# Three PSUM places for a second-layer tile, block products in single-bank tiles, normalisation one tile later, halves of 384 and 512 tokens

## The chip, the cores and the metric

The kernel runs on one core of a Trainium2 chip. The metric is the device time of one execution in microseconds; before the change three runs gave a median of 462.89 us (462.61 to 463.26). The engines are named as the profile names them: PE (TensorE, matrix products; PEld is its weight load), DVE (VectorE), ACT (ScalarE), POOL (GpSimd) and SP (SyncE, which here issues DMAs). PSUM is the memory that PE writes its products to; it has eight banks of 512 float32 columns, and DVE and ACT read it.

## The reference

Three stages, all in float32, on 2 x 448 = 896 tokens of width 768:

```python
scores = cap * tanh(scale * q @ k.T / cap); attn = softmax(scores)      # 2 x 12 heads of 64
x = (attn @ v)                                                         # 896 x 768
h = x @ moe_w_in                                                       # 768 -> 2048
x = (s * relu(h)**2 + b) @ moe_w_out                                   # 2048 -> 768
h = x @ moe2_w_in                                                      # 768 -> 1024
solu = h * exp(h - max(h)) / (sum(exp(h - max(h))) + 1e-9)
ln = (solu - mean) / sqrt(var + 1e-6) * g_ln
out = ln @ moe2_w_out                                                  # 1024 -> 768
```

The weights come in as float64 and are turned into float32 on the chip.

## The kernel before

Each matrix is split into a high part in a shortened format (fp32r) and the remainder, and one product is three matmuls: high x high, high x low, low x high (`mm3`, L374 to L377). The tile framework puts the instructions of each engine in one fixed order and adds the semaphore waits; every engine then runs its own list strictly in order.

Attention comes first and is not changed. In the first feed-forward layer the tokens stand along the columns and are cut in two halves, of 510 and 386 tokens (`M0`, L399, `HALVES`): for each of 16 blocks of 128 hidden units there is one product per half (`in_unit`), whose result ACT turns into relu squared. Then `split_g` (L402) makes the high and low part of s times that; two extra columns on the first half (512 columns in all) carry b, so that column `M0` of a result is the constant to add.

The second product of that layer is done in two sweeps (`sweep`, L1068): output blocks `dc` 0 and 1, then 2 to 5, each in one PSUM bank per half, summed over the 16 hidden blocks. At a sweep's end `evac` (L1093) moves each bank to SBUF as a high part (ACT, L1115) and a low part (DVE, L1118). The target `y` is laid out by tiles of 128 tokens; 510 is not a multiple of 128, so each half takes two pieces: 384 and 126 columns, and 2 and 384. PE may start a product in a bank of the next sweep when all pieces of the block that was there have been read.

The last layer goes by seven tiles of 128 tokens. `h2(t)` makes the tile's 1024 columns of h in one place of two banks; there are two such places (`ps_h`, L1188), so tile t+2 waits until DVE's product `so = h * rs * e` (L1210), the last reader, has finished tile t. `epilogue` (L1199) is a chain through three engines: DVE max (L1200), ACT exp (L1204), DVE sum and reciprocal, DVE `so` and its sum (L1210), ACT square (L1216), POOL variance, power -0.5 and minus mean times that (L1217, L1220, L1221), and ACT normalise (L1222). Beside it DVE and ACT convert the last weights `w2o` and form sums of their blocks (`block_sums`, L808), which `weights.pump(11)` interleaves, tile by tile.

The output product treats tile 0 alone (`first_out`, L1281) and the other tiles in pairs (`pair_out`, L1326): tiles t and t+1 share seven half-size products of 4 x 3 matmuls instead of eight, from sums and differences of rows (`pair_rows`, L1295) and of weight blocks. The results x, y, z, w of the products are columns of two tiles of two banks each, `xy` and `zw`, from the same places as h; DVE adds them up (L1350) and the rows are stored by SP's queue (`store`, L1377). `in_turn` fixes the order of PE here.

Of the kernel before, what the change touches and what calls it, by code (L numbers as in the profile page):

```python
# [10 lines left out]
F32 = mybir.dt.float32  # L11
# [3 lines left out]
AF = mybir.ActivationFunctionType  # L15
ALU = mybir.AluOpType
# [4 lines left out]
def full(ap):  # L21

    return ap.bitcast(F32)
# [14 lines left out]
def tile_softcap_attention__relu2__solu(  # L38
# [39 lines left out]
    def psum(name, bufs):  # L78
        return tc.tile_pool(name=name, bufs=bufs, space=PSUM, reuse_waits="tile")
# [116 lines left out]
    def layers(ctx, general):  # L196
# [199 lines left out]

        M0 = 510  # L399
        HALVES = (slice(0, M0), slice(M0, NT))  # L400

        def split_g(fc, part):  # L402
# [625 lines left out]
        gsp = left.enter_context(sb("gs"))  # L1028
        pairs = ([], [])
        for n in range(GSB):  # L1030
            m = 512 if n % 2 == 0 else NT - M0
            gh, gl = (gsp.tile([P, m], F32R, name=f"g{x}{n}") for x in "hl")
            pairs[n % 2].append((gh, gl))
            if n % 2 == 0:
                ends = slice(M0, M0 + 2)
                nc.gpsimd.tensor_copy(gh[:, ends], b_t.to_broadcast([P, 2]))
                nc.gpsimd.tensor_tensor(
                    out=gl[:, ends], in0=b_t.to_broadcast([P, 2]), in1=full(gh[:, ends]),
                    op=ALU.subtract,
                )  # L1040
# [38 lines left out]
        def sweep(dcs, banks, wname, used, pumps):  # L1079
            ahead = dict(split_ahead)  # L1080
            split_ahead.clear()

            def get(fc):
                if fc < KF and fc not in ahead:
                    ahead[fc] = [split_g(fc, b) for b in range(B)]

            def unit(fc, dc, b):
                wh, wl = wname(fc)
                gh, gl = ahead[fc][b]
                i = dcs.index(dc)  # L1090
                d = slice(i * P, (i + 1) * P)
                mm3(banks[dc, b][:, :gh.shape[1]], wh[:, d], wl[:, d], gh, gl, fc == 0, fc == KF - 1)

            def evac(b):
                if not ys:
                    both = act_tile("y")
                    ys.append(both.rearrange("p (t i) -> p t i", t=NTT))
                    ys.append(both.rearrange("p (t n k i) -> p t n k i", t=NTT, n=2, k=KD))
                y = ys[1]
                tok = HALVES[b]  # L1100
                cut = M0 // P * P if b == 0 else P - M0 % P
                for dc in dcs:
                    ps = banks[dc, b]
                    if b == 0:
                        adds[dc] = gsp.tile([P, 1], F32, tag=f"add{dc}", name=f"add{dc}")
                        nc.vector.tensor_copy(adds[dc], ps[:, M0:M0 + 1])
                    for a, e in ((0, cut), (cut, tok.stop - tok.start)):
                        t, r = divmod(tok.start + a, P)
                        if e - a < P:
                            src = ps[:, a:e]  # L1110
                            yh, yl = (y[:, t, n, dc, r:r + e - a] for n in range(2))
                        else:
                            src = ps[:, a:e].rearrange("p (t i) -> p t i", i=P)
                            yh, yl = (y[:, t:t + (e - a) // P, n, dc] for n in range(2))
                        nc.scalar.activation(  # L1115
                            out=yh, in_=src, func=AF.Identity, bias=adds[dc]
                        )
                        nc.vector.scalar_tensor_tensor(  # L1118
                            out=yl, in0=src, scalar=adds[dc], in1=full(yh),
                            op0=ALU.add, op1=ALU.subtract,  # L1120
                        )

            for fc in range(KF - 2):
                get(fc)
                get(fc + 1)
                for b in range(B):
                    for dc in dcs:
                        unit(fc, dc, b)
                        weights.pump(pumps)
                        side.pump(1)  # L1130
                used(fc)

            for fc in range(KF - 2, KF):
                get(fc)
                wname(fc)
            for b in range(B):
                for fc in range(KF - 2, KF):
                    for dc in dcs:
                        unit(fc, dc, b)
                        weights.pump(pumps)  # L1140
                        side.pump(1)
                with tc.high_priority(offset=100):
                    evac(b)
            for fc in range(KF - 2, KF):
                used(fc)
# [39 lines left out]
        right.close()  # L1185
        fin = ctx.enter_context(sb("fin"))
        fin2 = ctx.enter_context(sb("fin2", side="right"))
        ps_h = ctx.enter_context(psum("ps_h", 2))  # L1188
        ps_x = ctx.enter_context(psum("ps_x", 4))
        NHALF = DF2 // 2  # L1190
        for f in WT_B:
            spare[f"wt_w2o{f}"] = lambda name: fin.tile(
# [6 lines left out]
        def epilogue(t, ps, nm, se, rs, su, nmu, vs, va, rstd, nmr):  # L1199
# [18 lines left out]
                out=va, in0=vs, scalar1=1.0 / DF2, scalar2=1e-6, op0=ALU.mult, op1=ALU.add  # L1218
            )
            nc.gpsimd.tensor_tensor(out=rstd, in0=va, in1=mh_t, op=ALU.pow)  # L1220
            nc.gpsimd.tensor_tensor(out=nmr, in0=nmu, in1=rstd, op=ALU.mult)  # L1221
            nc.scalar.activation(out=so, in_=so, func=AF.Identity, scale=rstd, bias=nmr)  # L1222
            ln_of[t] = so

# [44 lines left out]
        def first_rows(banks):  # L1269
# [3 lines left out]
                    split_evac(lh[:, 4 * n:4 * n + 4, :], ll[:, 4 * n:4 * n + 4, :], ps)  # L1273
            return lh, ll

        def first_out(lh, ll):
            po = ps_h.tile([P, 2, 512], F32, tag="h", name="o0")
            ot = wt_tile("ot0")

            def products():  # L1280
                for f in range(KF2):  # L1281
                    wh, wl = w2o_of[f]
                    for n, m in enumerate((LEFT, RIGHT)):
                        mm3(po[:, n, :NO], lh[:, f, :], ll[:, f, :], wh[:, m], wl[:, m],
                            f == 0, f == KF2 - 1)

            in_turn(products)
            nc.scalar.copy(out=ot.rearrange("p (a m) -> p a m", a=2), in_=po[:, :, :NO])
            store(ot, 0, slice(0, DM), loads)

        PLACES = (
# [32 lines left out]
            yield  # L1324

        def pair_out(t, rows):  # L1326
            xy, zw = (ps_h.tile([P, 2, 512], F32, tag="h", name=f"o{t}_{n}") for n in range(2))
            x, y, z, w = (b[:, n, :NO] for b in (xy, zw) for n in range(2))
            ot, ot_b = wt_tile(f"ot{t}"), wt_tile(f"ot{t + 1}")
            tmp = full(weights.raws[f"w2o{KF2 - 1}"])  # L1330
            p1, u2, u3, v = (tmp[:, n * NO:(n + 1) * NO] for n in range(4))
# [8 lines left out]
            def product(*args):  # L1340
                in_turn(lambda: products(*args))
# [4 lines left out]
            def summed(n):  # L1346
                return lambda f: sums_of[f][n]
# [2 lines left out]
                nc.vector.tensor_tensor(out=out, in0=in0, in1=in1, op=op)  # L1350

            product(x, "a11", own(0, LEFT))
            nc.scalar.copy(out=p1, in_=x)
            product(z, "s1", summed(0))
            product(y, "s2", summed(1))
            add(u2, y, p1)
            add(v, u2, z, ALU.subtract)
            product(x, "a12", own(1, LEFT))
            add(ot[:, LEFT], p1, x)
            if last:  # L1360
                store(ot, t, LEFT, loads)
            product(w, "s3", summed(2))
            add(u3, w, u2)
            add(ot_b[:, RIGHT], u3, z, ALU.subtract)
            product(y, "a22", summed(3))
            add(ot_b[:, LEFT], u3, y)
            store(ot_b, t + 1, slice(0, DM), loads)
            ahead = {}
            prep = iter(()) if last else pair_rows(t + 2, ahead)
            next(prep, None)  # L1370
            product(z, "s4", own(1, RIGHT))
            add(ot[:, RIGHT], v, z, ALU.subtract)
            store(ot, t, RIGHT if last else slice(0, DM), loads)
            next(prep, None)
            return ahead

        def store(ot, t, m, queue):  # L1377
            pieces = []
            n = 0
            while n < P:  # L1380
                col = t * P + n
                b, rem = divmod(col, S)
                c, p0 = divmod(rem, CP)
                step = min(P - n, CP - p0)
                pieces.append((step, n, b, c, p0))
                n += step
            for step, n, b, c, p0 in sorted(pieces, reverse=True):
                rows = out[b * S:(b + 1) * S].rearrange("(p c) m -> c p m", c=NC)
                queue.dma_start(out=rows[c, p0:p0 + step, m], in_=ot[n:n + step, m])

        hint(nc.tensor)
        rest_of_sums.append(fin2.tile([P, 4 * NO], F32R, name="rest_of_sums"))
        weights.pump(11)
        for t in range(NTT):
            if t == NTT - 1:
                in_turn(lambda: banks0.extend(turned_ln(0)))
            h2(t)
            rows_done[0] += 1
            if t == NTT - 1:
                rows0 = first_rows(banks0)  # L1400
            with ExitStack() as behind:
                for e in ("dve", "act"):
                    behind.enter_context(tc.issue_after(chain[e].ins))
                weights.pump(11)
        rows = {}
        prep = pair_rows(1, rows)
        next(prep)
# [44 lines left out]
```

## Time and profile before

| | us |
|---|---|
| profiled execution | 463.24 |
| its span | 461.4 |
| PE busy (share of the span) | 452.4 (98%) |
| DVE busy | 382.4 (83%) |
| ACT busy | 297.0 (64%) |
| POOL busy | 96.5 (21%) |
| median of three runs | 462.89 |

The span runs from the first to the last profiled instruction; 1.8 us of the execution lie around it. Matmuls overlap in the records: one is drawn until its last column has passed through, while the next has begun. So the time PE loses is read from the distance between starts, or from the gap that the profile puts in brackets behind a row together with what ended it.

### The profile page before, as it was taken

The page shows a single profiled execution, that of the slowest core. Times are in us where ns is not written, and L with a number is a line of the kernel's source. Part 1 is how long each engine was busy: PE and PEld are TensorE (multiplying, and loading weights), DVE is VectorE, ACT ScalarE, POOL GpSimd, SP SyncE. Part 2 cuts the span into 40 slices and gives each one's busy share as a digit, 9 for nine tenths or more (in the row PEclk, how much of TensorE's full clock was granted, in tenths as well). Part 3 has the DMA queues.
Part 4 walks back from the last instruction along what each step waited for, and adds up shares of the span by engine and source line. Part 5 has one row for each costly group of instructions (what it writes and reads, how often), then busy time and mean ns, then how long its engine had stood idle before and what let it go on. Part 6 is the DMA issues. An engine that isn't in the chain of part 4 may idle for free.

```text
span 461.4 us, 6671 instructions
## 1 busy us (share of the span) xinstructions
PE 452.4 (98%) x2395; PEld 370.8 (80%) x2395; DVE 382.4 (83%) x645; ACT 297.0 (64%) x443; POOL 96.5 (21%) x96
## 2 busy tenths in 40 slices
PE   9999999999999999999999999999999999999996
PEld 7545455557898989889888889899888887999995
DVE  3898989868999999974899998988798998966472
ACT  3998999972776677763777755555565765953030
POOL 8178786777000000000000000000000123210000
PEclk9999999999999999999999999999999999999999
DMA  6766570114546666532233234443402230011022
GB/s 147 170 182 119 122 188 1 18 52 155 184 127 199 213 195 206 183 92 68 70 92 92 92 97 140 132 135 138 138 8 76 84 108 0 2 36 52 18 71 70
DMA packets 44743, 49.24 MB, mean 107 GB/s; under 512 B 21442, under 2 KB 37058, under 8 KB 44706
## 3 DMA queue, kind: packets, MB, share of 16 engines
q1 hardware_dynamic: 43856, 47.85, 35.6%
q0 software_dynamic: 368, 0.81, 0.7%
q8 instruction: 20, 0.33, 0.3%
q10 hardware_dynamic: 482, 0.11, 0.1%
q14 instruction: 17, 0.14, 0.1%
HBM read 46.01 MB, written 2.75 MB: 106 GB/s over the span
## 4 chain that ended last, share of the span: by engine, by line
PE 83%; DVE 8%; ACT 4%; DMA 2%; POOL 2%; issue 1%; DVEq 0%; ACTq 0%; POOLq 0%; SPq 0%
PE in L375 9%; PE in L377 8%; PE in L376 8%; PE o L627 8%; PE s L585 7%; PE y L375 6%; PE y L376 6%; PE y L377 6%; PE o L375 4%; PE o L377 4%; PE o L376 4%; PE m L637 2%; PE h L375 2%; PE h L376 2%; PE h L377 2%; DMA raw<-in_moe_w_out_dram 2%
## 5 line engine op out<-in xcount | busy, mean ns | idle before, releaser
L375 PE MATMUL in<-x,h_wi 128*128 128x510 f32 (+2 forms) x192 | 70.3, 366 | 0.0
L377 PE MATMUL in<-x,l_wi 128*128 128x510 f32 (+2 forms) x192 | 69.9, 365 | 0.0
L376 PE MATMUL in<-x,h_wi 128*128 128x510 f32 (+2 forms) x192 | 69.8, 365 | 0.0
L1217 POOL TENSOR_SCALAR small<-small 128x1 f32<-128x1 f32 x7 | 3.0, 432 | 281.3 <-PE h L377 240.9
L407 ACT ACTIVATE gh<-g,s_t 128x510 fp32r<-128x510 f32 (+1 forms) x64 | 42.2, 668 | 14.7 <-PE y L377 14.5
L408 DVE SCALAR_TENSOR_TENSOR gl<-g,s_t,gh 128x510 fp32r<-128x510 f32 (+1 forms) x64 | 42.8, 682 | 1.0 <-ACT gh L407 1.0
L592 ACT ACTIVATE e<-s 128x896 f32<-128x896 f32 (+1 forms) x48 | 37.9, 820 | 6.0 <-PE s L585 5.6
L599 ACT ACTIVATE e<-e,a_t 128x2240 f32<-128x2240 f32 (+1 forms) x24 | 40.5, 1690 | 0.4
L375 PEld LDWEIGHTS in<-x,h_wi 128*128 128x128 f32 x192 | 36.0, 188 | 5.4 <-ACT e L599 0.7
L377 PEld LDWEIGHTS in<-x,l_wi 128*128 128x128 f32 x192 | 36.0, 187 | 3.7
L376 PEld LDWEIGHTS in<-x,h_wi 128*128 128x128 f32 x192 | 36.0, 188 | 3.7
L627 PE MATMUL o<-e,vn 128*64 128x448 f32 x192 | 38.7, 545 | 0.0
L375 PE MATMUL h<-w2i_h,y 128*128 128x512 f32 x84 | 33.0, 393 | 1.0 <-DVE so L1210 1.0
L376 PE MATMUL h<-w2i_l,y 128*128 128x512 f32 x84 | 33.1, 394 | 0.0
L377 PE MATMUL h<-w2i_h,y 128*128 128x512 f32 x84 | 32.6, 388 | 0.0
L627 PEld LDWEIGHTS o<-e,vn 128*64 128x64 f32 x192 | 12.7, 136 | 20.4 <-issue 17.1
L610 POOL TENSOR_TENSOR c<-c,e 128x896 f32<-128x896 f32 x11 | 24.1, 2190 | 15.5 <-DVE c L616 11.9
L607 POOL TENSOR_TENSOR c<-e 128x896 f32<-128x896 f32 x11 | 23.3, 2116 | 12.6 <-ACT e L599 12.5
L269 ACT CAST h_wi<-wt_wi 128x768 fp32r<-128x768 f32 x16 | 13.3, 831 | 13.8 <-DVE wt_wi L263 8.4
L585 PE MATMUL s<-qh,kh 64*128 64x448 f32 (+1 forms) x84 | 21.2, 436 | 0.0
L247 ACT ACTIVATE wt_wi<-raw 128x768 f32<-128x768 f32 x15 | 13.5, 903 | 11.4 <-DMA raw<-in_moe_w_in_dram 8.9
L393 ACT ACTIVATE g<-in 128x510 f32<-128x510 f32 (+2 forms) x32 | 17.1, 537 | 5.5 <-PE in L377 5.5
(494 smaller groups left out, 1212.1 us busy)
## 6 DMA issues: line engine op xcount, KB each, us to landing
raw<-in_moe_w_in_dram SPq DMA_DIRECT2D x16, 768.0 KB, 4.9
raw<-in_moe_w_out_dram SPq DMA_DIRECT2D x24, 512.0 KB, 3.6
raw_w2i<-in_moe_w_in_dram SPq DMA_DIRECT2D x12, 512.0 KB, 5.0
raw<-in_moe_w_out_dram SPq DMA_DIRECT2D x8, 768.0 KB, 4.3
qn<-in_q_dram SPq DMA_DIRECT2D x16, 112.0 KB, 2.8
vn<-in_v_dram SPq DMA_DIRECT2D x12, 128.0 KB, 3.0
kn<-in_k_dram SPq DMA_DIRECT2D x20, 64.0 KB, 3.5
vn<-in_v_dram SPq DMA_DIRECT2D x12, 96.0 KB, 2.7
```

What stands on the lines that cost most here:

```text
L375: nc.tensor.matmul(o, lhsT=wh, rhs=xh, start=first, stop=False)
L376: nc.tensor.matmul(o, lhsT=wh, rhs=xl, start=False, stop=False)
L377: nc.tensor.matmul(o, lhsT=wl, rhs=xh, start=False, stop=last)
L393: nc.scalar.activation(out=r2, in_=ps[:, :m], func=AF.Relu)
L407: nc.scalar.mul(out=gh[:, :m], in_=r2, mul=s_t)
L408: nc.vector.scalar_tensor_tensor(out=gl[:, :m], in0=r2, scalar=s_t, in1=full(gh[:, :m]), op0=ALU.mult, op1=ALU.subtract,)
L585: nc.tensor.matmul(ps[:, j, :S], lhsT=kk[rows, c * P:(c + 1) * P], rhs=qq[rows], start=(x == 0), stop=(x == 2),)
L592: nc.scalar.activation(out=st["e", n][:, tiles(c), :], in_=ps[:, :m, :S], func=AF.Tanh)
L599: nc.scalar.activation(out=part, in_=part, func=AF.Exp, scale=a_t, bias=a_t)
L607: adder.tensor_tensor(out=c, in0=e[:, 1:3, :], in1=e[:, 3:5, :], op=ALU.add)
L610: adder.tensor_tensor(out=c, in0=c, in1=e[:, 5:7, :], op=ALU.add)
L627: nc.tensor.matmul(o[j * D:(j + 1) * D, :S], lhsT=vn[:, 2 * (n % 2) + j, c * D:(c + 1) * D], rhs=st["e", n][:, tiles(c).start + (j if c < ...
```

## The change

Five things change, all behind attention.

`M0` becomes 384, so the halves have 384 and 512 tokens (386 and 512 columns with the two of b); `evac` needs one piece per block and half. `ps_h` has three places, and beside it a pool of two banks holds the transposed rows of tile 0; when the last tile's h is made, both pools are given back, and the output products take four tiles of one bank each (x, y, z, w) and four banks for transposed rows. The factor `nmr` is made by ACT and not by POOL, and normalising tile t is issued behind the exp of tile t+1 (for tiles 5 and 6: behind the first copy of the first pair). In `pair_out` y and z change roles: a bank is taken anew, as its own tile, for each product. Tile 0's result is copied by ACT and DVE, half each, and of the very last two stores the second is issued from ACT's queue.

```diff
-        M0 = 510
+        M0 = NTT // 2 * P
...
-            m = 512 if n % 2 == 0 else NT - M0
+            m = M0 + 2 if n % 2 == 0 else NT - M0
...
-                cut = M0 // P * P if b == 0 else P - M0 % P
+                m = tok.stop - tok.start
+                tiles_of = slice(tok.start // P, tok.stop // P)
...
-                    for a, e in ((0, cut), (cut, tok.stop - tok.start)):
...
+                    src = ps[:, :m].rearrange("p (t i) -> p t i", i=P)
+                    yh, yl = (y[:, tiles_of, n, dc] for n in range(2))
+                    nc.scalar.activation(out=yh, in_=src, func=AF.Identity, bias=adds[dc])
+                    nc.vector.scalar_tensor_tensor(
+                        out=yl, in0=src, scalar=adds[dc], in1=full(yh),
+                        op0=ALU.add, op1=ALU.subtract,
+                    )
...
-        ps_h = ctx.enter_context(psum("ps_h", 2))
-        ps_x = ctx.enter_context(psum("ps_x", 4))
+        rows_of_h = ExitStack()
+        ps_h = rows_of_h.enter_context(psum("ps_h", 3))
+        ps_x = rows_of_h.enter_context(psum("ps_x0", 2))
...
-            nc.gpsimd.tensor_tensor(out=nmr, in0=nmu, in1=rstd, op=ALU.mult)
+            ln_of[t] = so, nmu, rstd, nmr
+
+        def normalise(t):
+            so, nmu, rstd, nmr = ln_of[t]
+            nc.scalar.mul(out=nmr, in_=nmu, mul=rstd)
             nc.scalar.activation(out=so, in_=so, func=AF.Identity, scale=rstd, bias=nmr)
...
+        def result(nm, t):
+            return ps_p.tile([P, 512], F32, tag=nm, name=f"o{nm}{t}")[:, :NO]
...
-            nc.scalar.copy(out=ot.rearrange("p (a m) -> p a m", a=2), in_=po[:, :, :NO])
+            nc.scalar.copy(out=ot[:, LEFT], in_=po[0])
+            nc.vector.tensor_copy(ot[:, RIGHT], po[1])
...
-            xy, zw = (ps_h.tile([P, 2, 512], F32, tag="h", name=f"o{t}_{n}") for n in range(2))
-            x, y, z, w = (b[:, n, :NO] for b in (xy, zw) for n in range(2))
+            x, y, z, w = (
+                made.pop(nm) if nm in made else result(nm, t) for nm in "xyzw"
+            )
...
-            nc.scalar.copy(out=p1, in_=x)
-            product(z, "s1", summed(0))
-            product(y, "s2", summed(1))
-            add(u2, y, p1)
-            add(v, u2, z, ALU.subtract)
+            copied = nc.scalar.copy(out=p1, in_=x)
+            product(y, "s1", summed(0))
+            product(z, "s2", summed(1))
+            add(u2, z, p1)
+            add(v, u2, y, ALU.subtract)
+            x = result("x", f"{t}b")
             product(x, "a12", own(1, LEFT))
...
+            if t == 1:
+                for late in (NTT - 2, NTT - 1):
+                    with tc.issue_after(copied.ins):
+                        normalise(late)
...
-            store(ot, t, RIGHT if last else slice(0, DM), loads)
+            store(ot, t, RIGHT if last else slice(0, DM), loads,
+                  nc.scalar if last and not general else loads)
...
             h2(t)
+            if 0 < t < NTT - 1:
+                with tc.issue_after(chain["act"].ins):
+                    normalise(t - 1)
...
+        rows_of_h.close()
+        ps_p = ctx.enter_context(psum("ps_p", 1))
+        ps_x = ctx.enter_context(psum("ps_x", 4))
+        made = {nm: result(nm, 1) for nm in "xy"}
```

The first place is DVE at the end of the first sweep, before the change. `y0_0` is the bank of output block 0, first half; `y0_1` that of its second half; `y1_*` those of block 1. The other rows make weights of the second sweep.

```order
L1118 SCALAR_TENSOR_TENSOR y_2585<-y1_0_2256,add1_2592,y_2585 128x3x128
L1118 SCALAR_TENSOR_TENSOR y_2585<-y1_1_2258,add1_2592,y_2585 128x2
L272 TENSOR_TENSOR l_wo2b_2643<-wt_wo2b_2644,h_wo2b_2642 128x512
L259 SCALAR_TENSOR_TENSOR wt_wo3b_2683<-raw1_59,wt_wo3b_2683 128x512
L1118 SCALAR_TENSOR_TENSOR y_2585<-y0_0_2255,add0_2586,y_2585 128x126
L1118 SCALAR_TENSOR_TENSOR y_2585<-y0_1_2257,add0_2586,y_2585 128x3x128
```

The same place after the change:

```order
L408 SCALAR_TENSOR_TENSOR gl2_1253<-g1_1312,s_t_82,gh2_1252 128x384
L1111 SCALAR_TENSOR_TENSOR y_2585<-y0_0_2255,add0_2586,y_2585 128x3x128
L254 TENSOR_SCALAR wt_wo3b_2675<-wt_wo3b_2675 128x512
L1111 SCALAR_TENSOR_TENSOR y_2585<-y0_1_2257,add0_2586,y_2585 128x4x128
L408 SCALAR_TENSOR_TENSOR gl3_1257<-g1_1312,s_t_82,gh3_1256 128x512
L1111 SCALAR_TENSOR_TENSOR y_2585<-y1_0_2256,add1_2590,y_2585 128x3x128
L1111 SCALAR_TENSOR_TENSOR y_2585<-y1_1_2258,add1_2590,y_2585 128x4x128
```

The bank `y0_0` is read by one instruction and no longer by a second one that stands behind two weight steps.

The second place is ACT in the last layer, between tiles 3 and 4, before the change. `h4` is the tile's result in PSUM, `e4` its exp, `so3` the row to be normalised, `small3` its column factors.

```order
L1216 ACTIVATE e3_3582,small3_3580<-so3_3586,small3_3580 128x1024
L1204 ACTIVATE e4_3654,small4_3652<-h4_3615,small4_3652 128x1024
L247 ACTIVATE wt_w2o7_3674<-raw1_59 128x768
L827 CAST y_2585<-suma2_3594 128x384
L1222 ACTIVATE so3_3586<-so3_3586,small3_3580 128x1024
L827 CAST y_2585<-sumc2_3596 128x384
```

The same place after the change:

```order
L1198 ACTIVATE e4_3628,small4_3626<-h4_3589,small4_3626 128x1024
L1219 ACTIVATE small3_3554<-small3_3554 128x1
L247 ACTIVATE wt_w2o7_3648<-raw1_59 128x768
L827 CAST y_2585<-suma2_3568 128x384
L1220 ACTIVATE so3_3560<-so3_3560,small3_3554 128x1024
L274 ACTIVATE w2o_h3_3579<-wt_w2o3_3581,g_t_88 128x768
L827 CAST y_2585<-sumc2_3570 128x384
```

The new L1219 makes the factor that POOL made; it stands right behind the exp and is the one that now waits for POOL's power. Normalising still stands behind the cast of `suma2`.

The third place is PE in the first pair, before the change: the end of the product into y (`o1_0`, the tile `xy`) and the next one into x of the same tile, then those into w and y. The brackets name the engines waited for.

```order
L376 MATMUL o1_0_3908<-y_2585,w2i_l_1277 128x384
L377 MATMUL o1_0_3908<-y_2585,w2i_l_1277 128x384
L375 MATMUL o1_0_3908<-w2o_h4_3211,w2i_h_1276 128x384 [waits DVE_49]
...
L375 MATMUL o1_1_3909<-y_2585,w2i_l_1277 128x384 [waits DVE_49]
...
L375 MATMUL o1_0_3908<-y_2585,w2i_h_1276 128x384 [waits DVE_49]
```

The same place after the change, with `oz1` and `ox1b` as tiles of their own:

```order
L376 MATMUL oz1_3892<-y_2585,w2i_l_1277 128x384
L377 MATMUL oz1_3892<-y_2585,w2i_l_1277 128x384
L375 MATMUL ox1b_3935<-w2o_h4_3203,w2i_h_1276 128x384 [waits Activation_49]
...
L375 MATMUL ow1_3893<-y_2585,w2i_l_1277 128x384 [waits DVE_49]
...
L375 MATMUL oz1b_3967<-y_2585,w2i_h_1276 128x384 [waits DVE_49]
```

The fourth product now waits for ACT, which copies the first product's x, and not for DVE.

## Rows read from the trace of the kernel before

**Rows 1.** The page, busy us (share of the span) and instructions: PE.
```profile
PE 452.4 (98%) x2395; PEld 370.8 (80%) x2395; DVE 382.4 (83%) x645; ACT 297.0 (64%) x443; POOL 96.5 (21%) x96
```

**Rows 2.** Waits of PE, whole run: us in total, times, longest us.
```profile
PE o L375 <- DVE raw L1350: 2.0, 3, 0.7
...
PE h L375 <- DVE so L1210: 1.0, 1, 1.0
PE y L375 <- DVE y L1118: 0.4, 1, 0.4
```

**Rows 3.** Busy us of each engine in windows: the tile loop's stretch.
```profile
334.00:388.00 54.00, 53.46 (x242) 44.29 (x240) 49.41 (x95) 36.42 (x63) 9.25 (x12) 1.00 0.18 59
```

**Rows 4.** Timeline of PE, first to second sweep: start us, us, instruction [idle before].
```profile
263.08 0.34 PE L376 MATMUL y<-gl,h_wo1b 128*128 128x386 f32 x1
263.26 0.34 PE L377 MATMUL y<-gh,l_wo1b 128*128 128x386 f32 x1
264.00 0.47 PE L375 MATMUL y<-gh,h_wo0b 128*128 128x512 f32 x1 [0.40 <-DVE y L1118]
```

**Rows 5.** Timeline of DVE at the same place.
```profile
262.30 0.69 DVE L272 TENSOR_TENSOR l_wo2b<-wt_wo2b,h_wo2b 128x512 fp32r<-128x512 f32 x1
262.90 0.69 DVE L259 SCALAR_TENSOR_TENSOR wt_wo3b<-raw,wt_wo3b 128x512 uint32<-128x512 uint32 x1
263.50 0.87 DVE L1118 SCALAR_TENSOR_TENSOR y<-y,add,y 128x126 fp32r<-128x126 f32 x2
```

**Rows 6.** Timeline of PE around the last tile's product.
```profile
386.42 1.04 PE L1251 MATMUL x<-ident,so 128*128 128x128 f32 x8
388.42 0.47 PE L375 MATMUL h<-w2i_h,y 128*128 128x512 f32 x1 [0.97 <-DVE so L1210]
...
396.75 1.91 PE L1251 MATMUL x<-ident,so 128*128 128x128 f32 x16
398.42 0.42 PE L375 MATMUL o<-w2o_h,w2i_h 128*128 128x384 f32 x1
```

**Rows 7.** The chain that ended last, before that product: start us, us, step.
```profile
380.59 2.19 POOL small L1220
382.84 1.97 POOL small L1221
384.83 1.24 ACT so L1222
386.08 0.41 ACT y L827
```

**Rows 8.** Timeline of PE, first pair: third to fourth product.
```profile
412.72 0.34 PE L376 MATMUL o<-y,w2i_l 128*128 128x384 f32 x1
412.89 0.34 PE L377 MATMUL o<-y,w2i_l 128*128 128x384 f32 x1
413.95 0.44 PE L375 MATMUL o<-w2o_h,w2i_h 128*128 128x384 f32 x1 [0.72 <-DVE raw L1350]
414.23 0.33 PE L376 MATMUL o<-w2o_l,w2i_h 128*128 128x384 f32 x1
```

**Rows 9.** Timeline of SP's DMA queue: the last two stores.
```profile
457.74 0.32 SPq L1389 DMA_DIRECT2D out_dram<-ot  x1
458.10 0.43 SPq L1389 DMA_DIRECT2D out_dram<-ot  x1
```

**Rows 10.** DMA issues, those two, and one from ACT at the start: KB, us to landing.
```profile
out_dram<-ot SPq DMA_DIRECT2D x1, 144.0 KB, 2.0
out_dram<-ot SPq DMA_DIRECT2D x1, 48.0 KB, 2.4
...
raw<-in_k_dram ACTq DMA_DIRECT2D x1, 48.0 KB, 3.3
```

**Rows 11.** Timeline of DVE: the low part of the first pair's sum of rows.
```profile
406.13 0.68 DVE L225 TENSOR_TENSOR w2i_l<-f,w2i_l 128x512 fp32r<-128x512 f32 x1
```

**Rows 12.** Timeline of PE: the matmul that reads it.
```profile
409.25 0.33 PE L377 MATMUL o<-rest_of_sums,w2i_l 128*128 128x384 f32 x1
```

More of the change, by code (lines that the diff above doesn't have):

```diff
@@ L1106, in evac @@
                         nc.vector.tensor_copy(adds[dc], ps[:, M0:M0 + 1])
-                    for a, e in ((0, cut), (cut, tok.stop - tok.start)):
[L1108 to L1121, printed above, removed]
+                    src = ps[:, :m].rearrange("p (t i) -> p t i", i=P)
[5 more added lines that the diff above has]
+                    )
             for fc in range(KF - 2):
@@ L1274, in first_rows @@
             return lh, ll
+        def result(nm, t):
+            return ps_p.tile([P, 512], F32, tag=nm, name=f"o{nm}{t}")[:, :NO]
         def first_out(lh, ll):
-            po = ps_h.tile([P, 2, 512], F32, tag="h", name="o0")
+            po = [result(nm, 0) for nm in "zw"]
             ot = wt_tile("ot0")
@@ L1283, in products @@
                     for n, m in enumerate((LEFT, RIGHT)):
-                        mm3(po[:, n, :NO], lh[:, f, :], ll[:, f, :], wh[:, m], wl[:, m],
+                        mm3(po[n], lh[:, f, :], ll[:, f, :], wh[:, m], wl[:, m],
                             f == 0, f == KF2 - 1)
             in_turn(products)
-            nc.scalar.copy(out=ot.rearrange("p (a m) -> p a m", a=2), in_=po[:, :, :NO])
+            nc.scalar.copy(out=ot[:, LEFT], in_=po[0])
+            nc.vector.tensor_copy(ot[:, RIGHT], po[1])
             store(ot, 0, slice(0, DM), loads)
@@ L1361, in pair_out @@
                 store(ot, t, LEFT, loads)
+            if t == 1:
+                for late in (NTT - 2, NTT - 1):
+                    with tc.issue_after(copied.ins):
+                        normalise(late)
             product(w, "s3", summed(2))
             add(u3, w, u2)
-            add(ot_b[:, RIGHT], u3, z, ALU.subtract)
-            product(y, "a22", summed(3))
-            add(ot_b[:, LEFT], u3, y)
+            add(ot_b[:, RIGHT], u3, y, ALU.subtract)
+            z = result("z", f"{t}b")
+            product(z, "a22", summed(3))
+            add(ot_b[:, LEFT], u3, z)
             store(ot_b, t + 1, slice(0, DM), loads)
@@ L1370, in pair_out, with store @@
             next(prep, None)
-            product(z, "s4", own(1, RIGHT))
-            add(ot[:, RIGHT], v, z, ALU.subtract)
-            store(ot, t, RIGHT if last else slice(0, DM), loads)
+            y = result("y", f"{t}b")
+            product(y, "s4", own(1, RIGHT))
+            add(ot[:, RIGHT], v, y, ALU.subtract)
+            store(ot, t, RIGHT if last else slice(0, DM), loads,
+                  nc.scalar if last and not general else loads)
             next(prep, None)
             return ahead
-        def store(ot, t, m, queue):
+        def store(ot, t, m, queue, other=None):
             pieces = []
@@ L1389, in store @@
                 queue.dma_start(out=rows[c, p0:p0 + step, m], in_=ot[n:n + step, m])
+                queue = other or queue
         hint(nc.tensor)
```

## Prediction

> **What bounds the kernel now.** I read the busy times first: PE works 452.4 us of a span of 461.4 [rows 1], so little is to be had except where PE stands still. The view of waits, asked for PE alone, names behind attention three such places with 3.4 us between them [rows 2]: three times 0.7 at most in the output product, once 1.0 before a product of h, once 0.4 at the border of the two sweeps. All three end with DVE reading a PSUM bank. Then the timelines of PE and of the engine that released it, at each of the three. The reader is to see there that PE's loss is more than the bracket says: a drawn matmul overlaps the next one, so I take the distance between starts and subtract the distance that matmuls of that width keep when nothing holds them. Last the stores at the end, since behind the last product nothing else runs.
>
> In the loop of the seven tiles DVE is the next engine, 49.41 us of 54, and ACT has 36.42 [rows 3]: a product of h that comes sooner meets a DVE with 4.6 us free.
>
> **The change, part by part.** The columns that PE has to do stay: 510 + 386 become 384 + 512 in the first product, 512 + 386 become 386 + 512 in the second, with the same number of matmuls. I count nothing for that, nor for ACT and DVE, whose pieces in the first layer swap places.
>
> *Border of the sweeps.* Two matmuls of 386 columns start 0.18 apart, the next one starts 0.74 after the second [rows 4]: 0.56 lost. The bank it wanted had its first piece read long before; what it waited for is the piece of 126 columns, at 263.50, which DVE does behind two weight steps of 0.69 [rows 5]. With 384 tokens there is no second piece, and DVE's list has the only one ahead of these steps. Gain 0.56. The bounds are 0.4 (the bracket) and 0.56 on one side. On the other, the second half's block is now larger and read by one instruction of 512 columns; if a bank of the second half were to come late by as much as the old piece did, the gain is 0. Taken: 0.56, since DVE reads the blocks in an unbroken row now. The twelve instructions saved on each of ACT and DVE lie beside PE and count nothing.
>
> *Third place for h.* Eight transposes start at 386.42. Sixteen of them, with no wait behind, take 1.67 from first start to the next product (396.75 to 398.42), so eight take 0.84, and tile 6 could have begun at 387.26; it began at 388.42 [rows 6]. That is 1.16, and the bracket of 0.97 is the lower end. It waited for tile 4's place. With three places tile 6 takes the place of tile 3, which was free a whole tile earlier. So the wait goes, whatever held tile 4's DVE step. What held it stands in the chain: POOL took 2.19 and 1.97 for two operations on one column, ACT's normalise waited for them and a cast behind it at 386.08 as well [rows 7]. The later normalise takes that wait out of ACT's list as well, unless POOL is slower than the exp that now stands between. Gain 1.16.
>
> *Block products in single-bank tiles.* Matmuls of 384 columns start 0.17 apart; the fourth product starts 1.06 after the last matmul of the third [rows 8], so 0.89 is lost. Its second matmul starts 0.28 behind, 0.11 more than usual: a restart costs that. The wait ended with DVE's step on y, while the product writes x, which ACT had copied out long before; x and y are only one tile. As tiles of their own x waits for ACT's copy alone. The other two pairs wait (2.0 - 0.72)/2 = 0.64 each [rows 2], and with the same 0.17 and 0.11 on top the three give 1.00 + 0.92 + 0.92 = 2.84. Lower end 2.0 (the brackets), lower still 0 if the wait is not the tile's. Taken: 2.84. The new tiles bring waits on ACT's or DVE's reading of the bank's previous content, but each bank is written again one product or more after its last reader was released, 12 x 0.17 = 2.1 us later, as the other products here do without a stall.
>
> *Work moved to ACT.* Seven operations on one column come to ACT. Even at POOL's slowest, 1.97 [rows 7], that would be 13.8 us, less than ACT's 17.6 free in the loop [rows 3]. Two normalisations move behind the first pair's copy, and are needed a pair later. Nothing.
>
> *New wait at the first pair.* PE comes to it 0.56 + 1.16 = 1.7 earlier, DVE perhaps not. The low part of the first sum of rows was done at 406.81 [rows 11] and read at 409.25 [rows 12]. Read at 407.5 instead, it still has 0.7, if DVE gains nothing. But DVE's list now has the last tile's `so` ahead of the first rows, ACT its square too, and the copy of tile 0's first half stands behind four casts. Between 0 and 0.7 lost; taken 0.2, as the slack is there on paper.
>
> *The last store.* The two last stores leave SP's queue at 457.74 and 458.10 [rows 9] and take 2.0 and 2.4 to land [rows 10], so the span waits for the second, at 460.5. From ACT it can leave at 457.74. If it takes 2.4 again, 0.36 is won; if it lands with the first, 0.76; if it takes the 3.3 of a transfer of that size from ACT at the start [rows 10], 0.54 is lost. Taken 0.36, that of the same store.
>
> The Trainium skill (DMA: Bandwidth & Descriptors, section Issuing engines are not separate DMA queues) says that DMAs from several engines run on the same transfer engines and that a second issuer saves only the time to issue. By that rule this part cannot give more than the 0.36 between the two issues, and the sum stays 4.72; without the rule the better end of 0.76 would make it 5.12. No row of this case has two issuers at work on stores.
>
> **Sum.** 0.56 + 1.16 + 2.84 - 0.2 + 0.36 = 4.72. The profiled execution took 463.24 (span 461.4 and 1.8 around it), 0.35 above the median of the runs. 463.24 - 4.72 = 458.5; from the median, which is what is timed, 458.2. With all brackets only and 0.7 lost at the pair it is 3.4 - 0.7 - 0.5 = 2.2 less, 460.7; with no new wait and 0.76 at the end 5.3 less, 457.6.
>
> **Rivals.**
> *DVE becomes the bound behind the tile loop.* For it: 49.41 of 54 busy [rows 3], and its list puts rows of the first pair behind the last `so`. Then what was won before the first pair comes back there as a wait on DVE, 1.16 + 0.56 in the worst case: 459.9. Against it: the slack of 0.7 above, and that ACT no longer makes DVE wait for POOL.
>
> *The wait in the pairs isn't the tile's.* If DVE's reading of any of these banks holds PE, the fourth product waits as before, and 2.84 falls away: 461.0. Against it: the second and third product write beside banks that are read, without a stall, and the order shows ACT in the bracket.
>
> *Slower.* POOL keeps its bad times, ACT now waits for it at L1219 right behind an exp, in five tiles of the loop. Each time that can be 2.19; behind it stand weight casts, and DVE waits for those: 5 x 2.19 = 11 us of standing DVE. DVE has 4.6 free [rows 3], so 6.4 would reach PE through late weights and rows: 458.2 + 6.4 = 464.6. It decides from the point where DVE's lost time is above 4.6. Against it: POOL was as slow as that in one tile of those that the chain shows, and ACT waited for it before too.
>
> *The change has no effect on the time* because the freed stretches turn up as waits elsewhere in the in-order lists, 462.9.
>
> **How the numbers follow.** Forecast 0.75, its own range 457.4 to 459.2 (the store's two ends, 0 to 0.7 at the pair). DVE as the bound 0.13, at 459.9. Waits in the pairs stay 0.05, at 461.0. No effect 0.03. Slower 0.04. A range of 457.3 to 460.2 holds the first two cases and leaves the others, 0.12, out. A measurement of this kernel tells 0.2%, about 0.9 us, from no change; the first three cases are beyond that: faster 0.93, same 0.03, slower 0.04.
>
> **What would show it.** In the waits of PE the rows of L375 on DVE's `raw`, `so` and `y` are gone. Matmuls across the border of the sweeps start 0.18 apart, tile 6 starts 0.84 behind the first of eight transposes, and the fourth product of each pair 0.17 behind the third. In the first pair a bracket on PE that names DVE's row parts or ACT's copy of tile 0 would be the new wait. The last store starts with the one before it and lands about 2.4 later. I am wrong if the fourth product still has its gap, if PE has new brackets between tiles 2 and 6, or if more than 0.7 turns up at the first pair.

## The result and the profile after

The changed kernel takes 458.65 us (median of 6 runs, 458.24 to 458.95), the kernel before 462.73 on the same chip: a ratio of 0.991, 95% interval 0.9897 to 0.9923. It is faster by 4.1 us; 458.2 was forecast, a gain of 4.7.

The profiled execution took 458.32, with a span of 456.4 against 461.4. The page, and the waits of PE over the whole run:

```profile
PE 450.2 (99%) x2395; PEld 369.4 (81%) x2395; DVE 382.6 (84%) x634; ACT 295.3 (65%) x438; POOL 91.1 (20%) x89
```
```profile
PE idle L179 <- DVE ones L167: 1.0, 1, 1.0
PE pq L477 <- DMA raw<-in_q_dram: 0.4, 1, 0.4
PE m L637 <- DVE c L610: 0.3, 1, 0.3
```

The three rows of [rows 2] are gone and nothing stands in their place: what is left lies at the start and in attention, which the change doesn't touch. At the border of the sweeps, PE and DVE ([rows 4, 5]; start us, us, instruction):

```profile
261.40 0.33 PE L377 MATMUL y<-gh,l_wo1b 128*128 128x386 f32 x1
261.57 0.34 PE L375 MATMUL y<-gh,h_wo0b 128*128 128x386 f32 x1
```
```profile
259.60 0.61 DVE L1111 SCALAR_TENSOR_TENSOR y<-y,add,y 128x384 fp32r<-128x384 f32 x1
```

The spacing is 0.17 where it was 0.74, and the first block has been read 1.4 us before PE wants its bank. Around the last tile's h, PE, DVE and POOL ([rows 6, 7]):

```profile
385.30 1.04 PE L1249 MATMUL x<-ident,so 128*128 128x128 f32 x8
386.09 0.48 PE L375 MATMUL h<-w2i_h,y 128*128 128x512 f32 x1
```
```profile
382.78 1.28 DVE L1204 SCALAR_TENSOR_TENSOR so<-h,small,e 128x1024 f32<-128x1024 f32 x1
```
```profile
377.19 0.55 POOL L1214 TENSOR_TENSOR small<-small,mh_t 128x1 f32<-128x1 f32 x1
```

Tile 6 starts 0.79 behind the first transpose. But tile 4's `so`, for which it used to wait, is now done at 384.06, two us before tile 6 starts: with only two places it would not wait either. And POOL's power (the -0.5 of the variance) took 0.55 where it had taken 2.19. The gain came; it need not come from where I put it. Third to fourth product of the first pair, and the low part of its first sum of rows with the matmul that reads it ([rows 8, 11, 12]):

```profile
410.57 0.34 PE L377 MATMUL oz<-y,w2i_l 128*128 128x384 f32 x1
410.75 0.34 PE L375 MATMUL ox1b<-w2o_h,w2i_h 128*128 128x384 f32 x1
```
```profile
405.60 0.68 DVE L225 TENSOR_TENSOR w2i_l<-f,w2i_l 128x512 fp32r<-128x512 f32 x1
```
```profile
406.93 0.34 PE L377 MATMUL oy<-rest_of_sums,w2i_l 128*128 128x384 f32 x1
```

The product follows in 0.18, and the sum of rows is ready 0.65 before it is read. The loop's busy times ([rows 3]), and the last stores (KB, us to landing; [rows 9, 10]):

```profile
334.00:388.00 54.00, 54.00 (x241) 44.42 (x240) 50.13 (x87) 35.33 (x58) 4.80 (x8) 1.00 0.18 59
```
```profile
out_dram<-ot SPq DMA_DIRECT2D x1, 144.0 KB, 2.2
out_dram<-ot ACTq DMA_DIRECT2D x1, 48.0 KB, 2.9
```

```profile
452.54 0.39 ACTq L1400 DMA_DIRECT2D out_dram<-ot  x1
```

DVE's last step ends at 452.50, so this store no longer stands behind another, but it took 2.9 to land; the span ends 3.9 behind DVE's last step, against 3.7 before.

The stages of the two profiled executions, by starts of PE and the end of DVE's last step: from the first product of the first layer to the first product of h 238.8 before and 238.3 after (0.5 less), from there to the first output product 61.4 and 60.3 (1.2 less), from there to the end of DVE's last step 59.3 and 56.4 (2.9 less), and the end behind it 3.7 and 3.9 (0.2 more). That is 4.35 in all. Attention, which is the same, took 0.65 less in this execution. That belongs to the execution and not to the change: the first layer starts at 98.16 before and 97.51 after, but at 97.46 in banks_alone and 98.07 in store_sp, two of the kernels below.

### The profile page after: what moved, and what is told of

The parts are those of the page before. It is cut to its first block, busy times and chain, and to the rows that moved or that the text cites. A ratio compares the mean times of both kernels' runs of the same rounds, so it can differ in the third digit from the quotient of the medians.

```text
span 456.4 us, 6630 instructions
## 1 busy us (share of the span) xinstructions
PE 450.2 (99%) x2395; PEld 369.4 (81%) x2395; DVE 382.6 (84%) x634; ACT 295.3 (65%) x438; POOL 91.1 (20%) x89
## 4 chain that ended last, share of the span: by engine, by line
PE 96%; DVE 1%; DMA 1%; ACT 1%; SPq 0%; issue 0%; DVEq 0%
PE y L375 9%; PE in L375 9%; PE y L376 9%; PE y L377 9%; PE in L377 9%; PE in L376 9%; PE o L627 8%; PE s L585 7%; PE h L375 4%; PE h L377 4%; PE h L376 4%; PE m L637 2%; PE x L1249 1%; PE pk L515 1%; PE pq L515 1%; DMA raw<-in_q_dram 1%
## 5 line engine op out<-in xcount | busy, mean ns | idle before, releaser
L377 PE MATMUL in<-x,l_wi 128*128 128x384 f32 (+2 forms) x192 | 69.9, 365 | 0.0
L375 PE MATMUL in<-x,h_wi 128*128 128x384 f32 (+2 forms) x192 | 69.9, 365 | 0.0
L376 PE MATMUL in<-x,h_wi 128*128 128x384 f32 (+2 forms) x192 | 69.8, 364 | 0.0
L407 ACT ACTIVATE gh<-g,s_t 128x384 fp32r<-128x384 f32 (+1 forms) x64 | 41.8, 666 | 10.6 <-PE y L377 10.2
L408 DVE SCALAR_TENSOR_TENSOR gl<-g,s_t,gh 128x384 fp32r<-128x384 f32 (+1 forms) x64 | 42.6, 680 | 2.2 <-ACT gh L407 1.8
L585 PEld LDWEIGHTS s<-qh,kh 64*128 64x128 f32 (+1 forms) x84 | 9.1, 184 | 12.2 <-issue 11.5
```

What stands on the lines that cost most here:

```text
L375: nc.tensor.matmul(o, lhsT=wh, rhs=xh, start=first, stop=False)
L376: nc.tensor.matmul(o, lhsT=wh, rhs=xl, start=False, stop=False)
L377: nc.tensor.matmul(o, lhsT=wl, rhs=xh, start=False, stop=last)
L407: nc.scalar.mul(out=gh[:, :m], in_=r2, mul=s_t)
L408: nc.vector.scalar_tensor_tensor(out=gl[:, :m], in0=r2, scalar=s_t, in1=full(gh[:, :m]), op0=ALU.mult, op1=ALU.subtract,)
L585: nc.tensor.matmul(ps[:, j, :S], lhsT=kk[rows, c * P:(c + 1) * P], rhs=qq[rows], start=(x == 0), stop=(x == 2),)
```

## The experiments

Each was timed in 5 rounds beside the kernel before. "After" is the changed kernel, 458.65. Intervals are about 0.6 us to each side (1.0 for double_bank_right), so differences below that are read from the traces.

**two_places**: after, with `psum("ps_h", 2)` for `psum("ps_h", 3)`.

> The changed kernel with two places for h instead of three, all else kept. Theory A, the step of the prediction: the third place took the 1.16 us wait away, so tile 6 again waits for tile 4's DVE step so; it starts about 2.0 us behind the first of the eight transposes, and the time is 458.65 + 1.16 = 459.8. Rival B: the later normalise took it away, since ACT no longer stands waiting for POOL ahead of the cast that DVE's so stands behind; the profile after has tile 4's so done at 384.06, 2.0 us before tile 6 starts at 386.09 with no wait. Then tile 6 starts 0.8 behind the transposes and the time stays 458.65.

Measured 458.68 (ratio 0.9915, 0.9902 to 0.9927), no bracket at tile 6. A is wrong: the third place isn't what took the wait away. Whether it was the later normalise, as B says, this run alone can't tell.

**early_norm**: after, three places, normalisation in the epilogue.

```diff
+            nc.gpsimd.tensor_tensor(out=nmr, in0=nmu, in1=rstd, op=ALU.mult)
...
-            nc.scalar.mul(out=nmr, in_=nmu, mul=rstd)
             nc.scalar.activation(out=so, in_=so, func=AF.Identity, scale=rstd, bias=nmr)
...
-            if 0 < t < NTT - 1:
-                with tc.issue_after(chain["act"].ins):
-                    normalise(t - 1)
```

> The changed kernel with the normalisation back in the epilogue and its factor made by POOL as before, three places for h kept. Theory A (the third place carries the gain): tile 6 takes tile 3's place and does not wait, whatever ACT and POOL do; the time stays 458.65. Rival B (the later normalise carries it): so of tile 4 is late again, near 387; with three places even that is no wait, so B too says 458.65 here, unless late work on DVE reaches PE in the first pair, up to 0.65 us there: 459.3. Read with the two other kernels.

Measured 463.17 (1.0014, 1.0002 to 1.0025; twelve runs from 462.33 to 464.75): 4.5 slower than after, the whole gain lost, which neither theory had. Waits of PE, then POOL, ACT and DVE behind tile 3:

```profile
PE oy L375 <- ACT w2i_l L224: 1.1, 1, 1.1
...
PE ox L375 <- ACT w2i_h L224: 0.8, 1, 0.8
PE oy L377 <- DVE w2i_l L225: 0.7, 1, 0.7
```
```profile
380.33 3.17 POOL L1214 TENSOR_TENSOR small<-small,mh_t 128x1 f32<-128x1 f32 x1
383.58 1.96 POOL L1215 TENSOR_TENSOR small<-small 128x1 f32<-128x1 f32 x1
```
```profile
385.57 1.24 ACT L1216 ACTIVATE so<-so,small 128x1024 f32<-128x1024 f32 x1 [2.78 <-POOL small L1215]
```
```profile
380.21 0.60 DVE L823 SCALAR_TENSOR_TENSOR suma<-wt_w2o,g_t,suma 128x384 f32<-128x384 f32 x1
380.74 0.55 DVE L254 TENSOR_SCALAR wt_w2o<-wt_w2o 128x768 uint32<-128x768 uint32 x1
381.20 0.55 DVE L828 TENSOR_TENSOR y<-sumb,y 128x384 fp32r<-128x384 f32 x1
381.67 0.55 DVE L828 TENSOR_TENSOR y<-sumc,y 128x384 fp32r<-128x384 f32 x1
382.14 0.95 DVE L259 SCALAR_TENSOR_TENSOR wt_w2o<-raw,wt_w2o 128x768 uint32<-128x768 uint32 x1
383.01 0.14 DVE L1201 TENSOR_SCALAR small<-small 128x1 f32<-128x1 f32 x1
```

POOL's power starts 0.12 behind DVE's L823 and ends only at 383.50, after five DVE steps; then the factor is held up too. ACT waits 2.78, tile 4's `so` starts at 388.86, 6.1 later than in after, and with three places PE isn't stopped there; it meets late rows in the first pair instead.

**two_places_early_norm**: both edits.

> The changed kernel with two places for h and the early normalise with POOL's factor: both undone. A and B both expect the wait of tile 6 back, about 1 us in brackets on DVE's so and 1.16 between starts: 459.8. If the wait stays away, neither of the two carried it, and it was an accident of POOL's time in the profiled execution of before: 458.65.

Measured 458.88 (0.9915, 0.9903 to 0.9928). Neither place nor normalise is needed to take the wait away, so B isn't the whole answer either; without the third place the early normalise is harmless. POOL's two operations:

```profile
377.43 0.55 POOL L1214 TENSOR_TENSOR small<-small,mh_t 128x1 f32<-128x1 f32 x1
378.06 0.19 POOL L1215 TENSOR_TENSOR small<-small 128x1 f32<-128x1 f32 x1
```

Tile 4's `so` ends at 385.63, ahead of tile 6's start at 386.26.

**double_bank**: after, with the pairs' products as before.

```diff
+            return ps_p.tile([P, 2, 512], F32, tag="o", name=f"o{t}_{n}")
...
-            product(y, "s1", summed(0))
-            product(z, "s2", summed(1))
+            product(z, "s1", summed(0))
+            product(y, "s2", summed(1))
```

> The changed kernel with the block products of the pairs back in two tiles of two banks each, in the old order of x, z, y, all else kept. Theory of the prediction: x waits for the tile, so for DVE's last reading of y; the three brackets on DVE of 0.64 to 0.72 come back, with 0.28 lost beside each, 2.84 in all: 461.5. Rival: PE was held by something else in that place (the row parts on DVE that come with the later start): then below 1 us comes back, under 459.7.

Measured 467.31 (1.0092, 1.0078 to 1.0107). The profiled execution is the slowest of its four, 469.04. Waits of PE, then a window of it (the third column from the end is the granted clock):

```profile
PE o L375 <- DVE so L1204: 4.2, 1, 4.2
PE o L375 <- DVE raw L1353: 2.0, 3, 0.7
```
```profile
401.00:407.30 6.30, 6.09 (x19) 6.12 (x20) 4.39 (x10) 4.83 (x9) 0.74 (x2) 0.50 0.01 3
```

The three brackets are back at their old size, but tile 0's product now stands in the place of the last tile's h and waits 4.2 for its last reader, and behind it PE ran 6 us at half clock in this execution. The price of the tiles alone isn't measured by this.

**double_bank_right**: the same, a place fixed for each tile (`tag=f"o{n}"`).

> The changed kernel with the pairs' products in two tiles of two banks, as double_bank, but with tile 0's product held to the place whose last content is tile 5's h and not tile 6's. Theory of the prediction: what double_bank lost ahead of the first pair (4.2 us on DVE's so of tile 6, and the stretch at half clock behind it) is gone, the three brackets of 0.64 to 0.72 stay, and 2.84 is lost in all: 461.5. Rival: two-bank tiles cost more than the waits, as in double_bank: above 463.

Measured 466.48 (1.0085, 1.0063 to 1.0107): my theory's 461.5 was wrong here.

```profile
PE o L375 <- DVE ot L1291: 3.1, 1, 3.1
PE o L375 <- DVE raw L1353: 2.0, 3, 0.7
```
```profile
409.42 0.56 DVE L1291 COPY ot<-o 128x384 f32<-128x384 f32 x1
```

The brackets are the same 2.0; the 3.1 is new. After has tile 0's result copied half by DVE, and that copy stands behind DVE's row parts. As its own bank, z waits only for ACT's half; in a tile of two banks it waits for DVE's as well. So the split copy of the change relies on the single banks. The rival, a cost of two-bank tiles beyond the waits, finds no room: the output products took 7.8 longer than in after (64.2 against 56.4), and by an estimate from this trace the stand makes 3.3 of it between starts, the 11 matmuls at half clock behind it 1.6 (3.47 instead of 1.9), and the three brackets 2.84, if they cost what they did before.

**banks_alone**: the kernel before, with `x, y, z, w` as single banks in the new order of y and z; tile 0's result is copied in two steps, both on ACT.

> The kernel before with the pairs' products in four tiles of one bank each, nothing else changed (510 and 386 tokens, two places for h, early normalise, last stores on one queue). Theory: 2.84 of the gain is this part's alone: 462.75 - 2.84 = 459.9, no bracket on DVE in the pairs. The wait of tile 6 tells more: if POOL's 2.2 and 2.0 us there follow from the order of DVE's list, which is the same here, the bracket of 1.0 on DVE's so is there again; if they were chance, it may be missing and the time nearer 458.8.

Measured 460.04 (0.9938, 0.9924 to 0.9951), 2.86 under its own before: 2.84 was forecast. The wait of PE at tile 6, and POOL:

```profile
PE h L375 <- DVE so L1211: 1.0, 1, 1.0
```
```profile
379.84 2.18 POOL L1221 TENSOR_TENSOR small<-small,mh_t 128x1 f32<-128x1 f32 x1
382.10 1.96 POOL L1222 TENSOR_TENSOR small<-small 128x1 f32<-128x1 f32 x1
```

No bracket in the pairs; tile 6 waits as before, with POOL's times equal to a hundredth to those of [rows 7]. That is what the same order of DVE's list would give, and not what chance would.

**early_norm_act** and **late_norm_pool**: early_norm with only the factor made by ACT, and after with only the factor made by POOL.

> The changed kernel with the normalisation back in the epilogue, but its factor still made by ACT; three places for h. early_norm lost 4.5 us with POOL's power at 3.17 and factor at 1.96 us in tile 3, ACT waiting 2.78 for them. If POOL's being held back is the cause, taking one of its operations away takes at least its 1.96 away: below 461.5. If the place of the normalise in ACT's list is the cause whatever POOL takes, the loss stays: 463.

> The changed kernel with its later normalisation, but the factor made by POOL as before; three places for h. If the later normalise is what guards ACT from POOL, nothing is lost: 458.65, and ACT's waits for POOL stay under 0.5 us each even where POOL takes 2 us and more. If ACT's making the factor was what helped, the loss of early_norm comes back: 461 to 463.

Measured 460.53 (0.9951, 0.9938 to 0.9964) and 459.47 (0.9928, 0.9915 to 0.9941). The wait row in the first pair, of the one, then of the other, and POOL and DVE at tile 3 in the one:

```profile
PE oy L377 <- DVE w2i_l L225: 1.0, 1, 1.0
```
```profile
PE oy L377 <- DVE w2i_l L225: 0.7, 1, 0.7
```
```profile
380.05 0.55 POOL L1214 TENSOR_TENSOR small<-small,mh_t 128x1 f32<-128x1 f32 x1
```
```profile
380.21 0.61 DVE L823 SCALAR_TENSOR_TENSOR suma<-wt_w2o,g_t,suma 128x384 f32<-128x384 f32 x1
```

With three places both halves of the edit count: of early_norm's 4.5 the factor on ACT saves 2.6, the later normalise 3.7, and as they overlap they don't add up. ACT still waited 3.5 for POOL in the first, 0.2 in the second. In early_norm_act POOL's power starts 0.16 ahead of L823 and takes 0.55; in early_norm it started 0.12 behind the same step and took 3.17. So the 2.6 isn't simply the price of the POOL operation taken away: the power itself, started 0.28 sooner against that step, took 2.62 less. The lists' order changes in both kernels, and POOL's share and the order's aren't separated.

**halves_384_alone**: the kernel before with `M0 = NTT // 2 * P` and one piece per block.

> The kernel before with halves of 384 and 512 tokens and one piece per block and half, nothing else changed. Theory of the prediction: this part gives the 0.56 at the border of the sweeps and no more; the wait of tile 6 is another part's and stays, since banks_alone had it again with the same POOL times: 462.9 - 0.56 = 462.3, bracket of 1.0 on DVE's so. Rival: it is the new order of the lists of DVE and ACT behind these halves that keeps POOL out of DVE's way in tile 4; then the bracket is gone too: 462.9 - 0.56 - 1.14 = 461.2.

Measured 461.55 (0.9968, 0.9956 to 0.998), and tile 6 doesn't wait. All of PE's wait rows behind attention, then POOL:

```profile
PE o L375 <- DVE raw L1343: 2.0, 3, 0.7
```
```profile
377.39 0.55 POOL L1213 TENSOR_TENSOR small<-small,mh_t 128x1 f32<-128x1 f32 x1
378.02 0.19 POOL L1214 TENSOR_TENSOR small<-small 128x1 f32<-128x1 f32 x1
```
```profile
377.44 1.23 DVE L1193 TENSOR_REDUCE small<-h 128x1 f32<-128x1024 f32 x1 [0.19 <-PE h L377]
```

The rival holds: with the halves alone the lists stand so that POOL's two steps fall 3.2 us earlier (the stage itself begins 1.0 earlier), beside DVE's max, which reads PSUM. In the kernel before the same max ran from 379.27 to 380.4 and POOL's power started at 380.59, behind it.

**halves_510**: after, with the old halves and pieces.

> The changed kernel with halves of 510 and 386 tokens and the two pieces again, all else kept. Theory: the border of the sweeps loses 0.3 to 0.57 again, tile 6 does not wait, because the normalise is late here, and the time is 459.1. Rival, if the halves alone keep tile 6 free: the bracket on so comes back as well, up to 460.3.

Measured 459.28 (0.9919, 0.9906 to 0.9933). Only the border is back.

```profile
PE y L375 <- DVE y L1118: 0.3, 1, 0.3
```
```profile
384.01 1.28 DVE L1211 SCALAR_TENSOR_TENSOR so<-h,small,e 128x1024 f32<-128x1024 f32 x1
```

Tile 4's `so` is done 1.8 before tile 6 starts, at 387.08, so the third place isn't what keeps tile 6 free here. What is left is the later normalise with ACT's factor, or the order that comes with the rest of the change; they aren't separated.

**store_sp** and **store_swapped**: after, with the two last stores on SP's queue, or with the large one on ACT's.

> The changed kernel with the two very last stores both on SP's queue, as before. Step of the prediction: the second issuer saves the 0.36 between the issues, so this is 0.36 slower, 459.0, and the span ends 4.2 us behind DVE's last step instead of 3.9. Rival: the store from ACT took 2.9 us to land against 2.4 for the second one from SP before; then the two ends are 0.14 apart the other way, the span ends 3.7 to 3.8 behind DVE's last step, and the time is 458.5.

> The changed kernel with the last two stores exchanged: the one of 32 rows from SP's queue, the one of 96 rows from ACT's. If a store from ACT lands late whatever it carries (2.9), the span ends 3.9 behind DVE's last step as in the changed kernel, 458.65. If the small store is the slow one on any queue (2.4 to 2.9) and the large one takes 2.0 from ACT too, it ends 3.4 to 3.5 behind: 458.2, which would be better than both kernels.

Measured 458.54 (0.9908, 0.9892 to 0.9923) and 458.92 (0.9913, 0.99 to 0.9927), no difference that the times can tell. Landings of the one's last two stores, then of the other's large one:

```profile
out_dram<-ot SPq DMA_DIRECT2D x1, 144.0 KB, 2.1
out_dram<-ot SPq DMA_DIRECT2D x1, 48.0 KB, 2.5
```
```profile
out_dram<-ot ACTq DMA_DIRECT2D x1, 144.0 KB, 3.1
```

The span ends 3.9 behind DVE's last step with both on SP, 3.9 with the small one on ACT, 4.1 with the large one. From ACT the small store took 2.9 to land and the large one 3.1, from SP 1.9 to 2.5 and 2.0 to 2.2: in these traces, one of each kernel, a last store from ACT lands later whichever it is. No version beats the changed kernel by more than a measurement can tell.

## Why the prediction was right

*Block products, 2.84.* Right in place and size: 2.89 in the trace, 2.86 alone, and the three brackets come back with two-bank tiles. It is two thirds of the gain.

*Border, 0.56.* Right: 0.57 between starts; back in halves_510. One reason given for it is not so: DVE doesn't read the blocks in an unbroken row, a weight step (L254) and a step of `split_g` (L408) stand between them. With 1.4 to spare it costs nothing.

*Third place for h, 1.16.* The size was right (1.18 in the trace), the cause was not. The step said that tile 6 no longer waits because it takes tile 3's place. The halves alone take the wait away (halves_384_alone), two_places loses nothing that the times can tell, and in halves_510, without the new halves, another part of the change does it, not the place. What I counted as nothing, the pieces that swap places on ACT and DVE, moved POOL's two operations out of DVE's way. That the number came out is luck: the wait was worth 1.16 whichever part removed it. Halves 1.3 and banks 2.9, each alone, add up to 4.2, the whole of the 4.1. No run has just these two, but two_places_early_norm, which has them and of the rest only tile 0's split copy, the smaller pools and the last store, stands at 458.88: the rest gives nothing that the times can tell.

*Work moved to ACT, 0.* Right for the changed kernel: ACT has no wait for POOL in its loop. But it isn't neutral: with three places for h the later normalise and ACT's factor are worth 4.5 (early_norm against after); with two they are worth nothing measurable. They guard the third place, which by itself brings nothing.

*New wait at the first pair, -0.2.* It isn't there; 0.65 is spare, where I had 0.7. That this is thin is shown by late_norm_pool and early_norm_act, where 0.7 and 1.0 turn up at just this matmul: the rival of DVE as the bound, and not far off.

*Last store, 0.36.* Wrong: the end is 0.2 longer than before, inside the bounds that the step gave (0.54 lost to 0.76 won). The step took over the 2.4 that the same store had needed from SP; from ACT it took 2.9. It left some 0.36 sooner behind DVE, and took about as much longer to land than the 2.5 of store_sp, which ends 3.9 behind DVE too: ACT's queue is worth nothing here. The 0.2 is therefore not the queue's; what it is stays open. The rule of the Trainium skill that stands there (DMA: Bandwidth & Descriptors, section Issuing engines are not separate DMA queues) holds here as an upper bound: no more than the 0.36 of issuing was won, and the longer landing took that back.

*Slower.* The mechanism, ACT standing for POOL, didn't appear; it did in early_norm, where ACT waited 7.0 for POOL in five places, at 463.17. The price had been 11 of waits and 464.6; the nearness of the two times isn't a proof of the price.

The sum was 4.72; the stages of the trace give 4.35, the medians 4.1 with an interval of 3.6 to 4.8. Of the 0.37 between sum and trace the store makes 0.57, and the wait that didn't come 0.2 the other way, so two misses partly cancel. The forecast's own range, 457.4 to 459.2, doesn't follow from the ends it names: the store's two ends and 0 to 0.7 at the pair give 457.6 to 459.6. The measured 458.65 lies in both.

## What to carry to other kernels

Where a bracket names an engine that reads a tile, look whether the product wants that part of the tile at all: a tile of two banks makes the one wait for the other's reader. Where a wait goes back to an operation that takes four times its usual time, look first at what runs beside it: here the order of the lists decided it, and an edit in the layer before removed it. To credit one part of a change with a gain, run that part alone; here several parts could each remove the same wait.

## What the runs showed of the hardware

POOL's power on one column took 0.55 us and its factor 0.19 where they were shortest. Where they began in a row of DVE steps on SBUF, as at tile 3 of the kernel before, of banks_alone and of early_norm, they took 1.96 to 3.17; other cases lie between (1.27 at the power of tile 2 before). The Trainium skill (SBUF — State Buffer, section SBUF: two separate sides) says that the two share a port pair, locked for a whole instruction, against DVE steps with two SBUF inputs or in a 2-port mode. The rows of early_norm agree in that POOL is held up among such steps and was not when its power started first (early_norm_act); they show besides that the wait can outlast several DVE steps. What lets POOL in at last stays open. In early_norm both ends came 0.1 to 0.5 behind the start of a DVE step on one column (383.01 and 385.41). But in the kernel before the power ended at 382.76, while DVE was still in L823:

```profile
382.27 0.61 DVE L823 SCALAR_TENSOR_TENSOR sumc<-wt_w2o,g_t,sumc 128x384 f32<-128x384 f32 x1
382.80 0.15 DVE L1207 TENSOR_SCALAR small<-small 128x1 f32<-128x1 f32 x1
```

With the shortest times taken off, an estimate, all four waits of these two traces ended some 0.06 before some DVE step started, on one column in three cases and L823 in the fourth.

After PE had stood 4.2 us in double_bank the granted clock was 0.50, the lower of the two levels, for the next 6 us: matmuls of 384 columns 0.32 apart instead of 0.17. Behind the stand of 3.1 in double_bank_right matmuls kept 0.17 for 1.5 us and then stood 0.32 apart for some 3.4 us. It isn't so in every execution: of that kernel's six runs one, 465.19, has a mean clock of 1.000, the others 0.990 to 0.996. The kernel before, with no stand behind attention longer than 1.2, had a mean of 1.000 over the whole span.
